# Moving two of seven block accumulations from VectorE to ScalarE and GpSimd in a fused attention and mixture-of-experts kernel

## The chip, the core and the metric

One core of a Trainium2 chip runs the whole kernel. The metric is the device time of that core in microseconds (us), as the median of several executions; lower is better. The short names of the profile are used throughout: PE is TensorE, PEld its weight loads, DVE is VectorE, ACT is ScalarE, POOL is GpSimd, SP the engine that issues most transfers.

## The reference

```python
def _attn_ref(q, k, v):                       # [8, 8, 576, 64] each
    q_p, k_p = phi(q), phi(k)                 # phi(x) = elu(x) + 1
    kv = np.einsum('bhsd,bhse->bhde', k_p, v)
    z = np.sum(k_p, axis=2)
    num = np.einsum('bhsd,bhde->bhse', q_p, kv)
    den = np.einsum('bhsd,bhd->bhs', q_p, z)[..., None] + 1e-06
    return num / den

def _moe_ref(x, w_gate, w1, w2):              # x 4608 x 512, 8 experts, F = 1024
    P = ...                                   # exp(logits), 8 rounds of row and column scaling
    out = np.zeros((N, D))
    for e in range(E):
        h = np.maximum(x @ w1[e], 0.0)
        ye = h @ w2[e]
        out += P[:, e:e + 1] * ye
    return out
# ... x is the attention's result, reshaped to 4608 x 512
```

## The kernel before

The attention runs in 16 groups, while its inputs are loaded. Then come 72 units: eight experts, nine groups of 512 tokens each. For experts 1 to 7 (63 units) the second product `h @ w2` is made by a seven-product scheme for 2 x 2 blocks, which needs sums of blocks: `S` of `h` (four for a unit) and `T` of `w2` (four for an expert). Each unit has two halves (`sub(0)`, `sub(1)`). Each half makes seven products `m1` to `m7`, and after each of them an accumulation `ev` adds the product, times the routing weight, to the output accumulator. The four sums are one DVE operation each; I call them S1 to S4.

A planner in the program (not the hardware) sets the order of the instructions on every engine. Each piece of work is a task with an estimated duration, the tasks on which it depends, and the buffers that it takes (`acq`) or uses. A dependency that crosses engines costs 0.12 us in its estimates.

```python
class _Plan:                                  # LAT = 0.12
    def slot(t):                              # when are t's buffers free?
        r = t["ready"]
        for g in t["acq"]:
            o, n = g["pool"]["order"], g["pool"]["n"]
            if len(o) >= n:
                for u in o[len(o) - n]["users"]:
                    ...
                    r = max(r, d + self.LAT)
        return r
    # ... of the tasks that can start first, the one with the lowest "prio" is taken
    # ... a finished task makes its followers ready:
    c["ready"] = max(c["ready"], t["done"] + (0.0 if list(c["eng"]) == [e] else self.LAT))

def att(b, g):                                # one of 16 attention groups
    # ... v to fp16, two casts of 64 rows
    for hh in range(2):
        def f_v(e, hh=hh):
            s = slice(64 * hh, 64 * hh + 64)
            copy(e, gvv["tile"][s, :, :, hh, 0:D], gin["v"]["tile"][s])
        tvv.append(fadd({"pool": 1.35, "dve": 0.75} if n < 2 else ("pool", 1.35), f_v, ...))
    # ...
    tqa = fadd(("none", 0.0), f_qa, deps=[tph["q"]], acq=[gq], prio=pr)      # takes the buffer of q transposed
    # ...
        t1 = fadd(("pe", 0.06 * (j1 - j0)), f_qt, deps=[tph["q"]], acq=[gp], use=[gt["q"]], prio=pr)
    # ...
    txa = fadd(("none", 0.0), f_xa, deps=[tden], acq=[gxn], prio=pr)         # takes the buffer of the result
    # ...
        t1 = fadd(("pe", 0.12 * (i1 - i0)), f_num, deps=[tden], acq=[gn], use=[gq, gz], prio=pr)

def unit(e, g, gT, tT):
    # ... layer1: h = relu(x @ w1), on PE and ACT
    for i in range(4):                        # S1..S4, one DVE tensor_tensor of 128 x 1024 each
        a0, a1, op = [(h[:, 4:8, :, 1, :], h[:, 0:4, :, 1, :], ALU.add),
                      (Sx[:, 0], h[:, 0:4, :, 0, :], ALU.subtract),
                      (h[:, 0:4, :, 0, :], h[:, 0:4, :, 1, :], ALU.subtract),
                      (h[:, 4:8, :, 0, :], Sx[:, 1], ALU.subtract)][i]
        nc.vector.tensor_tensor(out=Sx[:, i], in0=a0, in1=a1, op=op)
    def sub(s):
        def ev(region, ti, dh, dep):
            g_, col = region
            gg = 4 * g + 2 * s + ti
            def f_e(_):
                dst = acc[g][:, 2 * s + ti, 256 * dh:256 * dh + 256]
                nc.vector.scalar_tensor_tensor(out=dst, in0=g_["tile"][:, col, :], scalar=P_sb[:, gg, e:e + 1],
                                               in1=dst, op0=ALU.mult, op1=ALU.add)
            # ...
        # m1 -> e1, m5 (S1) -> e5, m2 -> ev, m6 (S2) -> e6, m3 (S4) -> ev, m7 (S3) -> e7, m4 (waits for e7) -> ev
        if e == E - 1:
            for ti in range(2):
                out_dma(g, 2 * s + ti, ...)   # two transfers for each 128 tokens, all issued by nc.sync

def out_dma(g, tt, deps):
    for half in range(2):
        ...
        nc.sync.dma_start(out=dst, in_=acc[g][64 * half:64 * half + 64, tt, :])
```

The softmax here doesn't subtract the row's maximum and nothing guards it: scores larger than these inputs give would overflow.

Of the kernel before, what the change touches and what calls it, by code (L numbers as in the profile page):

```python
# [9 lines left out]
FP32 = mybir.dt.float32  # L10
FP16 = mybir.dt.float16
AF = mybir.ActivationFunctionType
ALU = mybir.AluOpType
# [3 lines left out]
class _Plan:  # L17
# [13 lines left out]
    def add(self, eng, fn, deps=(), prio=0.0, acq=(), use=(), lat=0.0, after=0.0):  # L31

        if isinstance(eng, tuple):
            eng = {eng[0]: eng[1]}
        k = len(self.t)
        t = {"eng": eng, "fn": fn, "prio": prio, "acq": tuple(acq), "lat": lat, "kids": [], "nd": 0,
             "ready": after, "done": None, "id": k}
        self.t.append(t)
        for d in set(x for x in deps if x is not None):
            self.t[d]["kids"].append(k)  # L40
            t["nd"] += 1
        for g in list(acq) + list(use):
            g["users"].append(k)
        return k

    def run(self):
        free, avail = {}, {}
        for t in self.t:
            for e in t["eng"]:
                free.setdefault(e, 0.0)  # L50
                avail.setdefault(e, [])
            if t["nd"] == 0:
                for e in t["eng"]:
                    avail[e].append(t)
        left = len(self.t)
        end = 0.0

        def slot(t):
            r = t["ready"]
            for g in t["acq"]:  # L60
                o, n = g["pool"]["order"], g["pool"]["n"]
                if len(o) >= n:
                    for u in o[len(o) - n]["users"]:
                        d = self.t[u]["done"]
                        if d is None:
                            return None
                        r = max(r, d + self.LAT)
            return r

        while left:  # L70
            best = None
            for e, lst in avail.items():
                te = None
                for t in lst:
                    r = slot(t)
                    if r is None:
                        continue
                    s = max(free[e], r)
                    if te is None or s < te:
                        te = s  # L80
                if te is None:
                    continue
                pick = None
                for t in lst:
                    r = slot(t)
                    if r is not None and r <= te + 1e-9 and (pick is None or (t["prio"], t["id"]) < (pick["prio"], pick["id"])):
                        pick = t
                if best is None or te < best[0]:
                    best = (te, e, pick)
            assert best is not None, "plan is stuck"  # L90
            te, e, t = best
            for x in t["eng"]:
                avail[x].remove(t)
            t["start"] = te
            t["on"] = e
            free[e] = te + t["eng"][e]
            t["done"] = free[e] + t["lat"]
            end = max(end, t["done"])
            for g in t["acq"]:
                g["pool"]["order"].append(g)  # L100
            t["fn"](e)
            left -= 1
            for k in t["kids"]:
                c = self.t[k]
                c["nd"] -= 1
                c["ready"] = max(c["ready"], t["done"] + (0.0 if list(c["eng"]) == [e] else self.LAT))
                if c["nd"] == 0:
                    for x in c["eng"]:
                        avail[x].append(c)
        return end  # L110
# [3 lines left out]
def kernel(  # L114
# [10 lines left out]
    nc = tc.nc  # L125
# [6 lines left out]
    P = 128  # L132
# [9 lines left out]
    S_ = _Plan()  # L142
    add = S_.add
# [12 lines left out]
    P_sb = const.tile([P, NTT, E], FP32, tag="Pn", name="P_sb")  # L156
    NA = 7
    acc = [const.tile([P, 4, 512], FP32, tag=f"acc{g}", name=f"acc{g}") for g in range(NA)] + [None] * (NG - NA)
# [10 lines left out]
    p_t = {n: S_.pool(2) for n in "kq"}  # L169
    p_vv, p_kvz, p_qpT, p_xn, p_rden = (S_.pool(2) for _ in range(5))  # L170
    p_att, p_hq, p_h = S_.pool(2), S_.pool(2), S_.pool(2)
    p_T, p_S = S_.pool(2), S_.pool(2)
    p_w1, p_w2 = S_.pool(2), S_.pool(2)
    p_ye = [S_.pool(1) for _ in range(4)]
# [27 lines left out]
    def fadd(*a, **kw):  # L202
        t = add(*a, **kw)
        front_ids.append(t)
        return t

    def att(b, g):
        n = 2 * b + g
        pr = n - 100.0
        src = [[NJ * D, P], [2 * S * D, 2], [1, NJ * D]]  # L210
        gin, tin, gt, tph = {}, {}, {}, {}
# [8 lines left out]
        for nm in "kq":  # L220
# [15 lines left out]
            def f_m(_, ge=ge, g_=gt[nm]):  # L236
# [5 lines left out]
                       acq=[gt[nm]], use=[gin[nm]], prio=pr)  # L242
# [6 lines left out]
        ta = fadd(("none", 0.0), f_va, deps=[tin["v"]], acq=[gvv], prio=pr)  # L249
        for hh in range(2):  # L250
            def f_v(e, hh=hh):
# [3 lines left out]
                            use=[gvv, gin["v"]], prio=pr))  # L255
        gkv, gz = S_.grp(p_att), S_.grp(p_kvz)
# [17 lines left out]
        gq = S_.grp(p_qpT)  # L274
# [3 lines left out]
        tqa = fadd(("none", 0.0), f_qa, deps=[tph["q"]], acq=[gq], prio=pr)  # L278
        tq = []
        for j0, j1 in ((0, 5), (5, NJ)):  # L280
            gp = S_.grp(p_att)

            def f_qt(_, j0=j0, j1=j1, gp=gp):
                gp["tile"] = aps.tile([P, 5, 2, PW], FP16, tag="att", name="qt_ps")
                for j in range(j0, j1):
                    nc.tensor.transpose(gp["tile"][:, j - j0, :, :].rearrange("p h w -> p (h w)"),  # L286
                                        gt["q"]["tile"][:, j, :, :].rearrange("p r d -> p (r d)"), ident)

            def f_qc(e, j0=j0, j1=j1, gp=gp):
                copy(e, gq["tile"][:, :, j0:j1, :].rearrange("p h j w -> p j h w"), gp["tile"][:, 0:j1 - j0])  # L290
            t1 = fadd(("pe", 0.06 * (j1 - j0)), f_qt, deps=[tph["q"]], acq=[gp], use=[gt["q"]], prio=pr)
            tq.append(fadd({"act": 0.12 + 0.113 * (j1 - j0), "dve": 0.2 + 0.057 * (j1 - j0)}, f_qc, deps=[t1, tqa],
                           use=[gp, gq], prio=pr))
        js = [0, 2, 4, 6, 7]
# [15 lines left out]
        tden = fadd(("pe", 0.35), f_den, deps=tq + tz, acq=[gden], use=[gq, gz], prio=pr)  # L310
# [4 lines left out]
        txa = fadd(("none", 0.0), f_xa, deps=[tden], acq=[gxn], prio=pr)  # L315
        txn = []
        for i0, i1 in ((0, 2), (2, 4), (4, 5)):
            gn = S_.grp(p_att)

            def f_num(_, i0=i0, i1=i1, gn=gn):  # L320
                gn["tile"] = aps.tile([P, 2, 2, 2, D], FP32, tag="att", name="num_ps")
                for i in range(i0, i1):
                    for hh in range(2):
                        nc.tensor.matmul(gn["tile"][:, i - i0, :, hh, :],  # L324
                                         lhsT=gq["tile"][:, hh, js[i]:js[i] + 2, :].rearrange("p j w -> p (j w)"),
                                         rhs=gz["tile"][:, hh, :, 0:D], start=True, stop=True)

            def f_xn(_, i0=i0, i1=i1, gn=gn):
                nc.vector.tensor_tensor(  # L329
                    out=gxn["tile"][:, i0:i1], in0=gn["tile"][:, 0:i1 - i0].rearrange("p i r h e -> p i (r h) e"),  # L330
                    in1=grd["tile"][:, i0:i1, :, None].broadcast_to([P, i1 - i0, 4, D]), op=ALU.mult)
            t1 = fadd(("pe", 0.12 * (i1 - i0)), f_num, deps=[tden], acq=[gn], use=[gq, gz], prio=pr)
            txn.append(fadd(("dve", 0.1 + 0.28 * (i1 - i0)), f_xn, deps=[t1, trd, txa], use=[gn, grd, gxn], prio=pr))
        for c2 in range(2):
            gx = S_.grp(p_att)
# [9 lines left out]
            t1 = fadd(("pe", 0.3), f_xt, deps=txn, acq=[gx], use=[gxn], prio=pr)  # L345
# [81 lines left out]
    for b in range(B):  # L427
        att(b, 0)
        att(b, 1)
        if b % 2 == 1:  # L430
            logits(b // 2)
    p_done = sinkhorn()

    accp = []
# [11 lines left out]
    fin_prev = {}  # L446
# [87 lines left out]
    def unit(e, g, gT, tT):  # L534
        gw1, tw1, gw2, tw2 = w_t[e]
        ui = e * NG + g
# [3 lines left out]
        for i in range(4):  # L540
            def f_S(_, i=i):
                if i == 0:
# [9 lines left out]
                          use=[gh, gS], prio=ui - 399.0))  # L552
        def sub(s):
# [27 lines left out]
            def ev(region, ti, dh, dep):  # L581
                g_, col = region
                gg = 4 * g + 2 * s + ti

                def f_e(_):
                    dst = acc[g][:, 2 * s + ti, 256 * dh:256 * dh + 256]
                    nc.vector.scalar_tensor_tensor(out=dst, in0=g_["tile"][:, col, :], scalar=P_sb[:, gg, e:e + 1],  # L587
                                                   in1=dst, op0=ALU.mult, op1=ALU.add)
                t = add(("dve", 0.48), f_e, deps=[dep, fin_prev[(gg, dh)], p_done], use=[g_], prio=ui - 400.0)
                fin_prev[(gg, dh)] = t  # L590
                return t
# [63 lines left out]
```

## Time and profile before

| | before |
|---|---|
| time | 1053.62 us median of 2 runs (1053.1 to 1054.13) |
| span of the profiled execution | 1053.3 us |
| busy: PE / DVE / ACT / POOL | 1012.7 / 730.2 / 432.1 / 54.8 us |
| PE idle in 0 to 52 us | 26.5 us |
| one unit, experts 1 to 7 | 13.02 us |

The prediction below shows the lines and reads them. The front is, in what follows, the first 200 us or so, in which the attention is made and the inputs arrive.

### The profile page before, as it was taken

The numbers are of one execution on the slowest core, as the hardware profiler recorded it, in microseconds if no ns is written. First come the engines' busy times: TensorE is split into PE (matmuls) and PEld (weight loads), VectorE is DVE, ScalarE is ACT, GpSimd is POOL, SyncE is SP. The second block draws the span as 40 slices with busy tenths as digits, with TensorE's granted clock in tenths as the row PEclk, the third lists the DMA queues.
The fourth block names the chain that finished last, engine by engine and source line by source line (L and its number), as shares of the span: only waits on it lengthen the run. The fifth ranks groups of instructions, "written<-read, shape, count | busy, mean of one in ns | idle before, by whom it ended". The sixth has DMA issues, their size and how long they took to land.

```text
span 1053.3 us, 17028 instructions
## 1 busy us (share of the span) xinstructions
PE 1012.7 (96%) x7048; PEld 652.9 (62%) x7048; DVE 730.2 (69%) x1507; ACT 432.1 (41%) x693; POOL 54.8 (5%) x55
## 2 busy tenths in 40 slices
PE   2799999999999999999999999999999999999997
PEld 1455565456666666666666666666666666666664
DVE  6787876847666766667666766677666766666666
ACT  4666664453333333333333333333333333333331
POOL 3332310000000000000000000000000000000000
PEclk9999999999999999999999999999999999999999
DMA  9969600050001300050002200050003100014333
GB/s 270 326 193 248 198 6 2 1 81 2 1 1 26 56 1 1 1 81 1 1 1 41 41 1 1 1 81 1 1 1 49 32 2 1 1 28 89 83 82 81
DMA packets 31966, 55.63 MB, mean 53 GB/s; under 512 B 2704, under 2 KB 10896, under 8 KB 31888
## 3 DMA queue, kind: packets, MB, share of 16 engines
q1 hardware_dynamic: 18816, 37.76, 12.1%
q0 software_dynamic: 13072, 16.79, 9.9%
q8 instruction: 55, 0.90, 0.4%
q14 instruction: 23, 0.19, 0.1%
HBM read 61.88 MB, written 9.44 MB: 68 GB/s over the span
## 4 chain that ended last, share of the span: by engine, by line
PE 88%; DVE 7%; DMA 2%; ACT 1%; issue 1%; POOL 0%; SPq 0%; DVEq 0%; POOLq 0%; ACTq 0%
PE hq L467 45%; PE ye L576 36%; PE ye L497 4%; DMA vin<-in_v_dram 1%; DMA kin<-in_k_dram 1%; PE kv_ps L261 1%; DVE tk L239 1%; DVE xn L329 1%; DVE tq L239 1%; PE xt_ps L340 1%; PE qt_ps L286 1%; PE num_ps L324 0%; DVE ek L237 0%; DVE gs L389 0%; DVE kvz L195 0%
## 5 line engine op out<-in xcount | busy, mean ns | idle before, releaser
L471 ACT ACTIVATE h<-hq 128x512 f16<-128x512 f32 x576 | 343.4, 597 | 552.0 <-PE hq L467 551.8
L467 PE MATMUL hq<-xT,w 128*128 128x512 f16 x2304 | 556.2, 379 | 0.6 <-ACT h L471 0.6
L587 DVE SCALAR_TENSOR_TENSOR acc<-ye,P_sb,acc 128x256 f32<-128x256 f32 x882 | 396.7, 483 | 144.4 <-PE ye L576 144.4
L467 PEld LDWEIGHTS <-w 128*128 128x128 f16 x2304 | 223.9, 98 | 197.1 <-issue 1.9
L576 PEld LDWEIGHTS <-S 128*128 128x128 f16 x2016 | 197.0, 98 | 51.4 <-DVE S L550 2.2
L576 PE MATMUL ye<-T,S 128*128 128x256 f16 x1512 | 196.0, 273 | 1.2 <-DVE S L550 1.2
L576 PEld LDWEIGHTS <-h 128*128 128x128 f16 x1512 | 147.9, 98 | 58.1 <-ACT h L471 0.6
L550 DVE TENSOR_TENSOR S<-h 128x1024 f16<-128x1024 f16 x126 | 86.8, 689 | 115.4 <-ACT h L471 115.4
L576 PE MATMUL ye<-w,h 128*128 128x256 f16 x1008 | 130.8, 273 | 0.4 <-ACT h L471 0.4
L497 PE MATMUL ye<-w,h 128*128 128x512 f16 x288 | 69.7, 385 | 0.0
L576 PE MATMUL ye<-w,S 128*128 128x256 f16 x504 | 65.3, 273 | 0.2 <-DVE S L550 0.2
L576 PE MATMUL ye<-T,h 128*128 128x256 f16 x504 | 65.3, 273 | 0.1
L181 POOL DMA_DIRECT2D w<-in_moe_w_dram x16 | 13.3, 830 | 659.6 <-PE hq L467 624.3
L197 POOL CAST vv<-vin 64x1152 f16<-64x1152 f32 x32 | 40.2, 1257 | 98.7 <-PE kv_ps L261 49.5
L497 PEld LDWEIGHTS <-h 128*128 128x128 f16 x288 | 27.1, 100 | 27.5 <-issue 2.2
L550 DVE TENSOR_TENSOR S<-h,S 128x1024 f16<-128x1024 f16 x63 | 43.2, 686 | 0.0
L550 DVE TENSOR_TENSOR S<-S,h 128x1024 f16<-128x1024 f16 x63 | 42.9, 681 | 0.0
L261 PE MATMUL kv_ps<-vv,tk 128*128 128x260 f16 x144 | 22.5, 309 | 7.4 <-DVE qpT L195 5.0
L329 DVE TENSOR_TENSOR xn<-num_ps,rden 128x512 f16<-128x512 f32 (+1 forms) x48 | 26.5, 596 | 2.7 <-PE num_ps L324 1.9
L286 PE MATMUL qt_ps<-ident,tq 128*128 128x128 f16 x144 | 13.7, 235 | 14.1 <-DVE tq L239 11.0
L324 PE MATMUL num_ps<-kvz,qpT 128*128 128x128 f16 x160 | 16.0, 229 | 9.2 <-DVE xn L329 6.6
L226 ACT ACTIVATE ek<-kin 128x1152 f16<-128x1152 f32 x16 | 18.6, 1162 | 14.5 <-DMA kin<-in_k_dram 10.6
(60 smaller groups left out, 330.9 us busy)
## 6 DMA issues: line engine op xcount, KB each, us to landing
w<-in_moe_w_dram POOLq DMA_DIRECT2D x16, 1024.0 KB, 9.5
kin<-in_k_dram SPq DMA_DIRECT2D x16, 576.0 KB, 5.3
qin<-in_q_dram SPq DMA_DIRECT2D x16, 576.0 KB, 5.5
vin<-in_v_dram SPq DMA_DIRECT2D x16, 576.0 KB, 5.9
out_dram<-acc SPq DMA_DIRECT2D x72, 128.0 KB, 2.4
wg_sb<-in_moe_w_gate_dram POOLq DMA_DIRECT2D x1, 8.0 KB, 15.7
```

Of the source, the lines that this page charges most:

```text
L197: nc.gpsimd.tensor_copy(out=dst, in_=src)
L226: nc.scalar.activation(out=ge["tile"], in_=gin[nm]["tile"], func=AF.Exp)
L239: nc.vector.tensor_tensor(out=o, in0=o, in1=ge["tile"], op=ALU.max)
L261: nc.tensor.matmul(gkv["tile"], lhsT=gt["k"]["tile"][:, j, :, :].rearrange("p r d -> p (r d)"), rhs=gvv["tile"][:, :, j, :, :], start=(j = ...
L286: nc.tensor.transpose(gp["tile"][:, j - j0, :, :].rearrange("p h w -> p (h w)"), gt["q"]["tile"][:, j, :, :].rearrange("p r d -> p (r d)") ...
L329: nc.vector.tensor_tensor(out=gxn["tile"][:, i0:i1], in0=gn["tile"][:, 0:i1 - i0].rearrange("p i r h e -> p i (r h) e"), in1=grd["tile"][: ...
L467: nc.tensor.matmul(ghq["tile"], lhsT=gw1["tile"][:, c, ts(f, P)], rhs=xT[c][:, ds(512 * g, 512)], start=(c == 0), stop=(c == NDT - 1))
L471: nc.scalar.activation(out=gh["tile"][:, f, :], in_=ghq["tile"], func=AF.Relu)
L497: nc.tensor.matmul(gy[tt]["tile"], lhsT=gh["tile"][:, f, ds(P * tt, P)], rhs=gw2["tile"][:, f, :], start=(f == 0), stop=(f == NFT - 1))
L550: nc.vector.tensor_tensor(out=Sx[:, i], in0=a0, in1=a1, op=op)
L576: nc.tensor.matmul(g_["tile"][:, col, :], lhsT=lhs(kk), rhs=rhs(kk), start=(first and kk == 0), stop=(kk == 3), skip_group_check=True)
L587: nc.vector.scalar_tensor_tensor(out=dst, in0=g_["tile"][:, col, :], scalar=P_sb[:, gg, e:e + 1], in1=dst, op0=ALU.mult, op1=ALU.add)
```

## The change

The intent is to relieve DVE, the second busiest engine. Of the seven accumulations of a half unit, those of m5 and m3 (the second and fifth by program order) are split: ACT scales the product by the routing weight into a staging buffer in SBUF, and POOL adds that to the accumulator. The same change repairs two things in the planner: it counts a buffer pool that one task takes from twice, and it makes two kinds of attention tasks wait for the task that takes their buffer.

```diff
         def slot(t):
             r = t["ready"]
+            seen = {}
             for g in t["acq"]:
                 o, n = g["pool"]["order"], g["pool"]["n"]
-                if len(o) >= n:
-                    for u in o[len(o) - n]["users"]:
+                i = len(o) + seen.get(id(o), 0)
+                seen[id(o)] = i + 1 - len(o)
+                if i >= n:
+                    for u in o[i - n]["users"]:
@@
+    p_stage, ck = S_.pool(3), [0]
@@
-            t1 = fadd(("pe", 0.06 * (j1 - j0)), f_qt, deps=[tph["q"]], acq=[gp], ...
+            t1 = fadd(("pe", 0.06 * (j1 - j0)), f_qt, deps=[tph["q"], tqa], acq=[gp], ...
@@
-            t1 = fadd(("pe", 0.12 * (i1 - i0)), f_num, deps=[tden], acq=[gn], ...
+            t1 = fadd(("pe", 0.12 * (i1 - i0)), f_num, deps=[tden, txa], acq=[gn], ...
@@ def ev
+                ck[0] += 1
+                if ck[0] % 7 in (2, 5):
+                    gs_ = S_.grp(p_stage)
+
+                    def f_a(_):
+                        gs_["tile"] = accp[1].tile([P, 256], FP32, tag="stage", name="stage", bufs=3)
+                        nc.scalar.mul(out=gs_["tile"], in_=g_["tile"][:, col, :], mul=P_sb[:, gg, e:e + 1])
+
+                    def f_g(_):
+                        dst = acc[g][:, 2 * s + ti, 256 * dh:256 * dh + 256]
+                        nc.gpsimd.tensor_tensor(out=dst, in0=gs_["tile"], in1=dst, op=ALU.add)
+                    ta = add(("act", 0.5), f_a, deps=[dep, p_done], acq=[gs_], use=[g_], prio=ui - 400.0)
+                    t = add(("pool", 0.7), f_g, deps=[ta, fin_prev[(gg, dh)]], use=[gs_], prio=ui - 400.0)
+                    fin_prev[(gg, dh)] = t
+                    return ta
```

More of the change, by code (lines that the diff above doesn't have):

```diff
@@ L290, in f_qc @@
                 copy(e, gq["tile"][:, :, j0:j1, :].rearrange("p h j w -> p j h w"), gp["tile"][:, 0:j1 - j0])
-            t1 = fadd(("pe", 0.06 * (j1 - j0)), f_qt, deps=[tph["q"]], acq=[gp], use=[gt["q"]], prio=pr)
+            t1 = fadd(("pe", 0.06 * (j1 - j0)), f_qt, deps=[tph["q"], tqa], acq=[gp], use=[gt["q"]], prio=pr)
             tq.append(fadd({"act": 0.12 + 0.113 * (j1 - j0), "dve": 0.2 + 0.057 * (j1 - j0)}, f_qc, deps=[t1, tqa],
@@ L331, in f_xn @@
                     in1=grd["tile"][:, i0:i1, :, None].broadcast_to([P, i1 - i0, 4, D]), op=ALU.mult)
-            t1 = fadd(("pe", 0.12 * (i1 - i0)), f_num, deps=[tden], acq=[gn], use=[gq, gz], prio=pr)
+            t1 = fadd(("pe", 0.12 * (i1 - i0)), f_num, deps=[tden, txa], acq=[gn], use=[gq, gz], prio=pr)
             txn.append(fadd(("dve", 0.1 + 0.28 * (i1 - i0)), f_xn, deps=[t1, trd, txa], use=[gn, grd, gxn], prio=pr))
```

## The prediction

The 0.46 us of a staged copy (116 us in all, ACT about 548) is the 371 ns of the trace plus a term that is cut; without it the copies make 252 x 371 ns = 93 us and ACT 526, and the sum of the path stays 0. The 0.75 us of a POOL add (190 us, POOL about 245) came from terms that are all cut, so it was my estimate and not shown; the 0.6 to 0.75 us of blocking and the +13 to +35 us of the port rival, and through them the upper end of the range, rest on it. The point of 1053.5 us contains neither. The spacings of 215.8 and 109.2 ns are in the trace: in the unit after 621.08 us the matmuls start 215 to 216 and 109 to 110 ns apart. That they could not start sooner is not shown; what is shown is that PE has no gap to close there (200.00 us busy of 200). "The port" is my word for what the lines at 55.03 us show: the DVE sum ended 0.60 us after the end of a POOL cast (55.96 us) that had begun 0.41 us before it. That a port is the cause is not shown.

> **What bounds the kernel now.** I read the page's busy shares and slices first, then the busy times by stretch, then the chain of waits, then one unit in the timeline. One core runs, so there is one clock and no second die.
>
> The first lines of the page (engines, then the slices):
>
> ```profile
> PE 1012.7 (96%) x7048; PEld 652.9 (62%) x7048; DVE 730.2 (69%) x1507; ACT 432.1 (41%) x693; POOL 54.8 (5%) x55
> ...
> PE   2799999999999999999999999999999999999997
> ...
> PEclk9999999999999999999999999999999999999999
> ```
>
> TensorE is busy 96% of the span, at full clock; it idles in the first two slices and the last. A busy TensorE can still be a slow one, so I ask for stretches: columns are length, then busy us and instruction count of PE, PEld, DVE, ACT, POOL, then clock, DMA share and GB/s.
>
> ```profile
> 0.00:26.00 26.00, 6.99 (x47) 4.64 (x48) 17.78 (x31) 10.27 (x9) 7.95 (x13) 1.00 1.03 270
> 26.00:52.00 26.00, 18.54 (x141) 12.50 (x139) 19.24 (x36) 18.00 (x24) 9.94 (x8) 1.00 0.95 334
> ...
> 400.00:600.00 200.00, 200.00 (x1351) 132.05 (x1350) 137.77 (x285) 73.44 (x123) 3.28 (x4) 1.00 0.14 22
> 600.00:800.00 200.00, 200.00 (x1355) 132.49 (x1354) 136.62 (x283) 73.44 (x123) 1.64 (x2) 1.00 0.07 12
> ...
> 1030.00:1054.00 24.00, 15.71 (x113) 10.43 (x111) 13.50 (x29) 4.18 (x7) 0.00 (x0) 0.97 0.38 88
> ```
>
> From 200 us to the tail TensorE never idles. Its 40.6 us of idle time (1053.3 - 1012.7) are 26.5 in the first 52 us, where the DMA engines are full (share 1.03 and 0.95), about 6.5 from there to 200 us, and the rest in the tail. The chain of waits agrees: 88% PE, 7% DVE, 2% DMA. In the part that changes (63 units: experts 1 to 7, nine token groups each) the chain shows the start of each group of 12 first-layer matmuls at 256.69, 269.71, 282.73: 13.02 us for one unit.
>
> One unit in the timeline (start us, length us, engine, line, what, count, idle before):
>
> ```profile
> 623.64 0.69 DVE L550 TENSOR_TENSOR S<-h 128x1024 f16<-128x1024 f16 x1 [1.87 <-ACT h L471]
> ...
> 624.31 1.79 DVE L587 SCALAR_TENSOR_TENSOR acc<-ye,P_sb,acc 128x256 f32<-128x256 f32 x4
> 624.55 1.04 PE L576 MATMUL ye<-T,S 128*128 128x256 f16 x8
> ...
> 626.02 0.68 DVE L550 TENSOR_TENSOR S<-S,h 128x1024 f16<-128x1024 f16 x1
> ...
> 626.62 0.69 DVE L550 TENSOR_TENSOR S<-h 128x1024 f16<-128x1024 f16 x1
> 627.15 1.04 PE L576 MATMUL ye<-T,S 128*128 128x256 f16 x8
> 627.22 0.69 DVE L550 TENSOR_TENSOR S<-h,S 128x1024 f16<-128x1024 f16 x1
> ...
> 628.88 1.04 PE L576 MATMUL ye<-w,S 128*128 128x256 f16 x8
> ```
>
> These lines carry the argument. The four DVE sums S1 to S4 are made just ahead of the matmuls that load them: S4 ends at 627.91, its matmuls start at 628.88. Accumulations (L587) stand between S1 and S2.
>
> [...] A unit has 32 matmuls of 512 columns (215.8 ns) and 56 of 256 (109.2 ns): 6.91 + 6.11 = 13.02 us. The trace has exactly that, so a middle unit cannot become shorter, only longer. [...]
>
> ```profile
> 52.77 0.76 DVE L239 TENSOR_TENSOR tq<-tq,eq 128x1152 f16<-128x1152 f16 x1
> 53.41 2.54 POOL L197 CAST vv<-vin 64x1152 f16<-64x1152 f32 x2 [6.93 <-PE kv_ps L261]
> ...
> 54.46 0.46 DVE L237 TENSOR_SCALAR ek<-ek 128x1152 f16<-128x1152 f16 x1
> 55.03 1.54 DVE L239 TENSOR_TENSOR tk<-tk,ek 128x1152 f16<-128x1152 f16 x1
> ```
>
> The same two-input operation takes 0.76 us alone and 1.54 us beside a Pool cast. [...] No Pool add is in this trace; the one-input cast at 62.39 (two in 2.39 us) takes 1.19 us[...]. [...]
>
> **The change part by part.** Of seven accumulations per half unit two move, those of the products m5 and m3: 63 x 2 x 2 = 252.
>
> *Removed from DVE*: 252 x 483 ns (the L587 row) = 122 us; 730 becomes about 608 us. None of it is on the path: in the middle DVE waits for PE, not PE for DVE.
>
> *Added to ACT*: copies from PSUM take 585, 638 and 692 ns for 512, 576 and 640 columns, 0.836 ns a column, so 371 ns for 256[...]: about 0.46 us. 252 x 0.46 = 116 us; ACT becomes about 548 us (52%). It sits in gaps: ACT's 552 us of idle are waits for PE.
>
> *Added to Pool*: estimate [...]0.75 us; 252 x 0.75 = 190 us; Pool becomes about 245 us. Weight loads now stand behind adds in Pool's queue, but each weight has two buffers and an expert's time (9 x 13 = 117 us) against 9.5 us to land: hidden.
>
> *Moved order*. The compiled order shows more than the diff. In before a unit's TensorE order is m5, two first-layer groups, m6, one, m3, m7; in after one group stands before m6, so m6 and m3 come 0.87 us sooner after m5. On DVE, S1, four accumulations, S2, S3, S4 become S1, two accumulations, S2, S3, S4. Of the two repairs in the planner the repeated-slot count does nothing (no task takes two slots at once); the added dependencies reorder some attention work before 165 us, where I expect plus or minus 3 us.
>
> *The path of one unit*, with zero at the start of m5's pair and the gaps of the timeline: the two accumulations left run from -0.24 to 0.68, so S2 runs 0.60 to 1.28, S3 1.20 to 1.88, S4 1.80 to 2.48. m6 starts at 1.74 and m3 at 3.47; both are safe by 0.4 and 0.9 us. The staged copies start 0.63 (0.2 us after the product, as the L471 rows have it) and 1.07, end 1.1 and 1.55; m3, which overwrites that bank, waits for them and is safe by 1.9 us. Pool's two adds are ready near 1.2 and 1.9, just while S2 to S4 run. The sum of the planned parts on the path is therefore 0 for the middle. In the tail DVE is on the path (PE idles 1.18 us for S at 1043.25): two accumulations fewer before S2 are worth some 0.7 us, part of which the port may take back.
>
> **The rivals.** *The port becomes a wait.* If Pool's adds get in both between S2 and S3 and between S3 and S4 (each blocking some 0.6 to 0.75 us), S4 ends at 2.48 + 1.2 to 1.5 = 3.7 to 4.0, past 3.47: TensorE stalls 0.2 to 0.55 us a unit, 63 units: +13 to +35 us. For it: the lines at 55.03[...], and the packed order. Against it: the first add is ready only as S3 is being issued; if S3 wins, at most one add stands before S4, which then ends near 3.2, in time. I give the full form 3 chances in 10.
>
> *ACT becomes the bound or blocks TensorE.* A staged copy waits at the head of ACT's queue, with activations behind it. Against: 52% load, and the copies stand in the order in which TensorE finishes, with four banks for first-layer results. It would show as PE waiting for ACT; 1 in 20, some +5 us.
>
> *DVE relief pays.* DVE at 69% looks like a second bottleneck. Against: TensorE is at its rate in the middle, so nothing can be gained but in front and tail: 1 to 3 us, of 34 us idle which the input loads or the tail's data set. 2% would be 21 us.
>
> **Range and chances.** The central case is 1053.6 of before, minus about 0.5 in the tail, front unknown by 3: 1050 to 1056. To this comes the port rival with 3 in 10 and +13 to +35 us, its lower half inside the range that I state. Point 1053.5, range 1048.5 to 1068; faster by over 2% 0.01, slower by over 2% (over 0.33 us a unit) 0.13, the rest within.
>
> **What would show it right or wrong.** Right: counts DVE 1255, ACT 945, POOL 307; DVE near 608 us, unit spacing still 13.02 us, PE without idle between 200 and 1030 us. The steps: mean of an add near 0.75 us (longer if it is blocked), of the staged copy near 0.46 us; L550 above 0.69 us shows the port lock. Wrong: PE idle before the matmuls with S, released by DVE, some tenths of a us in each unit and a spacing above 13.2 us (the port), or released by ACT (the staged copy); or slices before 165 us whose PE busy time differs by more than 3 us (the reordered front).

## The result

| | before | after |
|---|---|---|
| time, us | 1053.62 (1053.1 to 1054.13, 2 runs) | 1058.12 (1057.27 to 1058.96, 2 runs) |
| span of the profiled execution, us | 1053.3 | 1057.2 |
| PE idle ahead of matmuls, us | 34.9 | 39.2 |
| DVE / ACT / POOL busy, us | 730.2 / 432.1 / 54.8 | 655.3 / 541.6 / 294.0 |

The ratio of the times is 1.0042, with a 95% interval from 1.0017 to 1.0066: the same within 2%, but a small, real loss. A ratio here is always the mean time of one kernel's fast runs over that of the other's of the same rounds, so it is not quite the ratio of the medians quoted.

The page of the kernel after: the engines' busy times with their instruction counts, then the first row of the slices.

```profile
PE 1011.4 (96%) x7048; PEld 652.7 (62%) x7048; DVE 655.3 (62%) x1251; ACT 541.6 (51%) x949; POOL 294.0 (28%) x307
...
PE   2699999999999999999999999999999999999996
```

DVE lost 75 us of work and nothing came of it: PE is as busy as before, with the same number of matmuls. The second slice and the last fell by one tenth each. So the loss is to be looked for mainly at the two ends.

Groups of the page of the kernel after, among its costliest: the columns are line, engine and operation, tiles, shapes and count, then busy us, mean ns of one, and the idle time before them.

```profile
L599 POOL TENSOR_TENSOR acc<-stage,acc 128x256 f32<-128x256 f32 x252 | 237.7, 963 | 546.7 <-ACT stage L595 546.7
...
L595 ACT ACTIVATE stage<-ye,P_sb 128x256 f32<-128x256 f32 x252 | 114.8, 475 | 52.1 <-PE ye L580 51.8
...
L554 DVE TENSOR_TENSOR S<-h,S 128x1024 f16<-128x1024 f16 x63 | 76.6, 1217 | 0.0
```

The last row is S4. On the page of the kernel before it is this row:

```profile
L550 DVE TENSOR_TENSOR S<-h,S 128x1024 f16<-128x1024 f16 x63 | 43.2, 686 | 0.0
```

Before it took 686 ns and 43.2 us in all, now 1217 ns and 76.6 us; S1, S2 and S3 stay between 679 and 694 ns. The extra 0.53 us falls on S4 alone, in every unit: its shortest record of 63 is 1214 ns, its longest 1220. The timeline of one unit of the kernel after shows why (start us, length us, engine, line, what, count, idle before):

```profile
627.89 1.04 PE L580 MATMUL ye<-T,S 128*128 128x256 f16 x8
628.50 0.68 DVE L554 TENSOR_TENSOR S<-S,h 128x1024 f16<-128x1024 f16 x1
...
629.10 0.68 DVE L554 TENSOR_TENSOR S<-h 128x1024 f16<-128x1024 f16 x1
629.14 2.35 POOL L599 TENSOR_TENSOR acc<-stage,acc 128x256 f32<-128x256 f32 x2 [8.14 <-ACT stage L595]
...
629.70 1.22 DVE L554 TENSOR_TENSOR S<-h,S 128x1024 f16<-128x1024 f16 x1
...
631.37 1.04 PE L580 MATMUL ye<-w,S 128*128 128x256 f16 x8
```

The staged copy frees POOL's first add at 629.14, 0.04 us after S3 has started. The add has to wait for S3, S4 has to wait for the add, and the second add waits for S4: the two engines take turns, in all 63 units (S4 ends 0.55 us after the end of the first add, the second add 0.58 to 0.59 us after the end of S4). (The prediction's lines at 55.03 us show the like between a DVE sum and a POOL cast, 1.54 us in place of 0.76; from here on it is called the lock on the port.) S4 ends at 630.92; its matmuls (m3, the last line) start at 631.37. So 0.45 us are left, no PE time is lost, and the units still start 13.02 us apart.

The tail is different. The timeline of the last unit of the kernel after, then the same part of the kernel before (the SPq line is the issue of eight output transfers):

```profile
1047.50 1.05 PE L580 MATMUL ye<-w,S 128*128 128x256 f16 x8 [0.69 <-DVE S L554]
1048.20 0.91 ACT L595 ACTIVATE stage<-ye,P_sb 128x256 f32<-128x256 f32 x2 [2.21 <-PE ye L580]
...
1048.76 1.41 POOL L599 TENSOR_TENSOR acc<-stage,acc 128x256 f32<-128x256 f32 x2 [0.73 <-ACT stage L595]
...
1049.51 4.96 SPq L486 DMA_DIRECT2D out_dram<-acc  x8
```

```profile
1044.32 2.58 DVE L587 SCALAR_TENSOR_TENSOR acc<-ye,P_sb,acc 128x256 f32<-128x256 f32 x6
1044.46 1.05 PE L576 MATMUL ye<-w,S 128*128 128x256 f16 x8 [0.16 <-DVE S L550]
1045.34 1.04 PE L576 MATMUL ye<-T,S 128*128 128x256 f16 x8
1045.62 4.97 SPq L482 DMA_DIRECT2D out_dram<-acc  x8
```

The eight matmuls with a weight as operand (`ye<-w,S`) are m3 of the last unit, both halves. From their start to the first output issue it takes 1045.62 - 1044.46 = 1.16 us before, when one DVE instruction lies between, and 1049.51 - 1047.50 = 2.01 us after, when an ACT copy and a POOL add do. From that issue on the two traces agree: eight issues in a row, 0.62 us each, and the end of the span 7.7 us after the first (1053.30 and 1057.16). The last issue waits for the seven ahead of it, not for the last accumulation, so a later first issue is a later end.

With gaps ahead of matmuls taken from the two traces, and the time after the last matmul (5.75 us before, 6.50 after), the difference of the spans, 3.9 us, is made up like this, as the gaps have it:

| part | after minus before, us |
|---|---|
| PE idle, 0 to 52 us | +3.5 |
| PE idle, 110 to 170 us | +0.7 |
| PE idle at the first unit with accumulations, near 243 us | +0.5 |
| PE idle in the tail | -0.2 |
| after the last matmul | +0.75 |
| PE's own busy time (1012.7 to 1011.4) | -1.3 |

The first and the last row belong together: the first 52 us hold 25.54 us of PE work before and 22.08 after, in a front with another order, and TensorE runs at half clock there for most of the time (matmuls of 128 columns 107 ns apart in place of 56, next section), so that busy and idle time say little by themselves. Starting times in the two traces give a sum without that. The first first-layer matmul starts at 44.08 us before and 45.86 after (+1.78). From it to the first routing matmul (`lg_ps`) both take 116.17 us. From there to the first first-layer matmul of the first unit with accumulations it is 71.96 and 72.89 (+0.93), from that to the next unit's 13.02 and 13.65 (+0.63), to the last unit nothing is added, and from the last S1 to the end it is 13.02 and 13.53 (+0.51). Together that is 3.85 of the 3.86 us.

### The profile page after: what moved, and what is told of

Read it like the earlier page. It is cut to its first block, busy times and chain, and to the rows that moved or that the text cites. A ratio compares the mean times of both kernels' runs of the same rounds, so it can differ in the third digit from the quotient of the medians.

```text
span 1057.2 us, 17661 instructions
## 1 busy us (share of the span) xinstructions
PE 1011.4 (96%) x7048; PEld 652.7 (62%) x7048; DVE 655.3 (62%) x1251; ACT 541.6 (51%) x949; POOL 294.0 (28%) x307
## 4 chain that ended last, share of the span: by engine, by line
PE 87%; DVE 9%; DMA 2%; issue 1%; ACT 1%; SPq 0%; DVEq 0%; ACTq 0%
PE hq L471 45%; PE ye L580 36%; PE ye L501 3%; DMA kin<-in_k_dram 2%; DVE tk L243 1%; DVE xn L333 1%; PE kv_ps L265 1%; PE xt_ps L344 1%; DVE tq L243 1%; PE qt_ps L290 1%; DVE ek L241 1%; DVE eq L241 1%; DVE S L554 0%; DVE tq L236 0%; DVE gs L393 0%
## 5 line engine op out<-in xcount | busy, mean ns | idle before, releaser
L599 POOL TENSOR_TENSOR acc<-stage,acc 128x256 f32<-128x256 f32 x252 | 237.7, 963 | 546.7 <-ACT stage L595 546.7
L607 DVE SCALAR_TENSOR_TENSOR acc<-ye,P_sb,acc 128x256 f32<-128x256 f32 x630 | 286.1, 481 | 166.2 <-PE ye L580 166.1
L595 ACT ACTIVATE stage<-ye,P_sb 128x256 f32<-128x256 f32 x252 | 114.8, 475 | 52.1 <-PE ye L580 51.8
L554 DVE TENSOR_TENSOR S<-h,S 128x1024 f16<-128x1024 f16 x63 | 76.6, 1217 | 0.0
L501 PEld LDWEIGHTS <-h 128*128 128x128 f16 x288 | 27.0, 100 | 27.1 <-issue 2.3
```

The lines of the kernel that those rows point to most:

```text
L501: nc.tensor.matmul(gy[tt]["tile"], lhsT=gh["tile"][:, f, ds(P * tt, P)], rhs=gw2["tile"][:, f, :], start=(f == 0), stop=(f == NFT - 1))
L595: nc.scalar.mul(out=gs_["tile"], in_=g_["tile"][:, col, :], mul=P_sb[:, gg, e:e + 1])
L599: nc.gpsimd.tensor_tensor(out=dst, in0=gs_["tile"], in1=dst, op=ALU.add)
```

## A second level in the times, which is not the change

Runs of one kernel fall on two levels some 1.5 us apart: among the experiments before took 1052.7 to 1053.4 or 1054.4 to 1054.6, after 1057.3 to 1057.6 or 1058.3 to 1059.0. A difference of one microsecond can be read only between runs of one level. The traces show what separates them. The timeline of the kernel after, profiled at 1058.96 us, and then that of the experiment off_only, profiled at 1054.15 us, at the same point of the program (L361 makes the routing logits, 8 columns a matmul):

```profile
167.79 2.84 PE L361 MATMUL lg_ps<-wg_sb,xT 128*128 128x8 f16 x108
170.50 5.30 PE L501 MATMUL ye<-w,h 128*128 128x512 f16 x16
```

```profile
165.54 2.85 PE L361 MATMUL lg_ps<-wg_sb,xT 128*128 128x8 f16 x108
168.24 3.61 PE L501 MATMUL ye<-w,h 128*128 128x512 f16 x16
```

The same 16 matmuls take 5.30 us or 3.61: 1.69 us. In the first case the clock records of the trace have 0.50 for 3.413 us, from 171.25 to 174.67 us, and 1.00 before and after; half the clock for 3.413 us is 1.71 us. It fell right after 108 matmuls of 8 columns in 2.85 us, in which PE shows no gap. Of 13 profiled executions, four have this stretch (before at 1055.08, after at 1058.96 and 1058.95, n0_split at 1051.71), each with 1.70 to 1.72 us lost by the granted clock; each is on the upper level of its kernel. The other nine do not have it, and those of them whose kernel showed two levels are on the lower.

That the narrow matmuls bring it about is my reading; no run took them away. The traces support it further. In each of them the recorded changes of the clock in mid-run lie whole multiples of 3.413 us, the length of the stretch itself, after the moment at which the full clock begins for good (before: 45.68 us, and 36 times 3.413 us later 168.56; after: 44.96 us, and 37 times later 171.25), so windows of this length can be counted from there. In the four executions with the stretch, the 108 narrow matmuls fill 2.56 to 2.71 us of the window just ahead of it; in the other nine they fall across the windows so that none has more than 2.34 us of them.

The traces show one thing more about the clock, which the clock column hides, because it reads 1.00 wherever no record exists. Two lines of timelines of the kernel before, five matmuls of 128 columns each:

```profile
39.61 0.74 PE L340 MATMUL xt_ps<-ident,xn 128*128 128x128 f16 x5
...
50.76 0.44 PE L340 MATMUL xt_ps<-ident,xn 128*128 128x128 f16 x5
```

In all 13 executions such matmuls stand some 107 ns apart until the full clock begins, at 42.5 to 47.7 us, and 56 ns apart after it; four executions have one window at full clock in between, near 25 to 31 us. So TensorE runs most of its first 42.5 to 47.7 us at half clock, in every kernel here.

The first profiles of before and after both have the stretch near 170 us, so the 3.9 us between their spans are not touched by it. In what follows I give the ratio over all fast runs, and beside it the medians of the lower level. For before that is 1053.0 us, for after 1057.5: a loss of 4.5.

## The experiments

Eleven kernels ran, beside the kernel before on the same chip, all correct. The theory after the result (A in the expectations) was: the change in the middle costs nothing, since the port takes back 0.53 us per unit that are not on the path; the loss comes from the reordered front (the two added dependencies) and, in smaller part, from the handoff ahead of the first output. The rival was that the offload itself costs the time somewhere.

### The offload alone, without the two dependencies: off_only

```diff
-            t1 = fadd(("pe", 0.06 * (j1 - j0)), f_qt, deps=[tph["q"], tqa], acq=[gp], ...
+            t1 = fadd(("pe", 0.06 * (j1 - j0)), f_qt, deps=[tph["q"]], acq=[gp], ...
-            t1 = fadd(("pe", 0.12 * (i1 - i0)), f_num, deps=[tden, txa], acq=[gn], ...
+            t1 = fadd(("pe", 0.12 * (i1 - i0)), f_num, deps=[tden], acq=[gn], ...
```

> The moved accumulations alone, with the planner's dependencies of the kernel before. Theory A (the loss is the planner's reordering of the front, plus a longer last handoff): front as before, S1 of the first unit near 233 us instead of 235.8, unit spacing 13.02 us, S4 at 1.22 us; only the tail is longer by about 0.5 us; time about 1054 to 1055, ratio to before 1.0005 to 1.001. Theory B (the offload itself costs, by the shared port): as the changed kernel, ratio 1.003 to 1.005.

Measured: 1054.25 us (1054.15 to 1054.53) against 1053.11 for before, ratio 1.0007 [0.9995, 1.002], by itself not told from no change. By the lower level it is +1.25. The front is back: PE idles 26.7 us in the first 52, as before (26.5), and the first first-layer matmul starts at 43.64 us (before 44.08, after 45.86). S4 still takes 1.216 us and units are still 13.02 us apart. The part of the loss that belongs to the offload shows in two places. One is the tail (5.88 us from the last S1 to the first output issue of the last group, before 5.34). The other is the first unit, in the timeline of off_only:

```profile
236.60 2.13 POOL L599 TENSOR_TENSOR acc<-stage,acc 128x256 f32<-128x256 f32 x2 [1.11 <-ACT stage L595]
236.94 1.22 DVE L533 TENSOR_TENSOR T<-w 128x1024 f16<-128x1024 f16 x1
...
238.60 0.60 PE L580 MATMUL ye<-T,h 128*128 128x256 f16 x4 [0.47 <-DVE acc L607]
```

Here a T sum of the weights falls beside the second pair of adds and is stretched from 0.68 to 1.22 us, the accumulation of m7 behind it comes late, and m4, which has to wait for that accumulation, costs PE 0.47 us. T is made once for an expert. The four sums at this place are those for expert 2, made back to back; those for the experts 3 to 7 stand 1.7 to 2.2 us apart, none takes over 0.80 us, and none makes a gap. By starting times this unit takes 13.65 us instead of 13.02, and from the last S1 to the end it is 13.54 instead of 13.02: with 0.63 and 0.52 us these two places hold 1.15 of the 1.25 us.

### The dependencies alone: deps_only

```diff
-            t1 = fadd(("pe", 0.06 * (j1 - j0)), f_qt, deps=[tph["q"]], acq=[gp], ...
+            t1 = fadd(("pe", 0.06 * (j1 - j0)), f_qt, deps=[tph["q"], tqa], acq=[gp], ...
-            t1 = fadd(("pe", 0.12 * (i1 - i0)), f_num, deps=[tden], acq=[gn], ...
+            t1 = fadd(("pe", 0.12 * (i1 - i0)), f_num, deps=[tden, txa], acq=[gn], ...
```

(The edit is on the kernel before; nothing else of the change is in.)

> The kernel before with both added dependencies and no offload. Theory A (the planner's reordering is most of the loss): ratio 1.002 to 1.0035, TensorE idle up by 1.7 to 3.5 us in the first 52 us and by 0.7 us from 110 to 170 us, no idle at the first unit, tail as before. Theory B (the offload is the loss): ratio 1.000.

Measured: 1055.91 us (1055.58 to 1057.4, 6 runs) against 1053.09, ratio 1.0027 [1.0015, 1.004]; lower level 1055.6, +2.6. PE idle in 0 to 52 us is 29.1 (before 26.5), in 110 to 170 it is 2.9 (2.2). So the repair of the planner, which adds no instruction at all, is the larger part of the loss: 2.6 of 4.5, the offload 1.25, and 0.6 stay that neither accounts for. In the traces these 0.6 us lie ahead of the first routing matmul, which starts at 161.46 us here and at 162.04 and 162.03 in the two traces of the kernel after, although the engines' order up to there is the same. The five traces with exactly the front's order of before spread from 159.58 to 160.25 at this point, so the 0.6 may be no effect of the change at all.

### Which group's dependency: txa_n0 and txa_rest

The compiled order had shown that the first dependency (on `tqa`) changes nothing and the second everything; the traces agree, for PE's order in deps_only is that of txa_rest with the exchange of txa_n0 at its beginning. These two runs ask in which of the 16 attention groups it costs.

```diff
 # txa_n0
-            t1 = fadd(("pe", 0.12 * (i1 - i0)), f_num, deps=[tden], acq=[gn], ...
+            t1 = fadd(("pe", 0.12 * (i1 - i0)), f_num, deps=[tden] + ([txa] if n == 0 else []), acq=[gn], ...
 # txa_rest: the same with n > 0
```

> The kernel before with the added dependency on the xn buffer for the very first attention group alone: in the compiled order it exchanges the first num_ps and the second kv_ps and nothing after. Theory A1 (that first exchange is what loses the front): first-layer work starts near 45.9 us instead of 44.1, time about 2 us over before (ratio 1.002). Theory A2 (the later reorderings at 80 to 165 us lose it): ratio 1.000.

Measured: 1054.85 us (1054.7 to 1056.34), ratio 1.0019 [1.0005, 1.0033]; lower level 1054.8, +1.8. PE idle in 0 to 52 us is 28.2, against 26.5; later stretches as before.

> The kernel before with the added dependency for all groups but the first: the order is as before until the eighth group, then differs. Theory A1: ratio 1.000 (within 0.7 us). Theory A2: about 2.5 us over before (ratio 1.0025).

Measured: 1053.54 us (1053.41 to 1055.27), ratio 1.0003 [0.9991, 1.0016]; lower level 1053.5, +0.5. Its idle in 110 to 170 us is 2.9 instead of 2.2, and the first 52 us are as before.

So one dependency in the first group costs most. What it does: `txa` is a task without an engine, and the planner adds its 0.12 us latency ahead of the followers. By that hair the second group's `kv_ps` wins a PSUM buffer over the first group's `num_ps`, and goes ahead of it on PE. Everything behind it shifts: the first first-layer matmul starts at 45.44 us; in the six traces without this exchange, and with the casts of before, it starts at 43.29 to 44.08. From there to the routing both kinds take the same 116.0 to 116.2 us.

### The offload, except in the last unit: off_notlast

```diff
 # on off_only
-                if ck[0] % 7 in (2, 5):
+                if ck[0] % 7 in (2, 5) and not (e == E - 1 and g == NG - 1):
```

> As off_only, but the last of the 63 units accumulates on DVE alone. If the tail's loss is the handoff from ACT to Pool ahead of the first output transfer of the last group, the output issues start 0.5 to 0.8 us earlier than in off_only relative to the last S1 (5.3 us after it as before, not 5.9), and time is that of before within 0.5 us. If the tail's loss is elsewhere, no difference to off_only.

Measured: 1053.76 us (1053.46 to 1055.14), ratio 1.0004 [0.9992, 1.0017]; lower level 1053.7, 0.5 below off_only. In the trace the interval from the last S1 to the first output issue is 5.34 us, exactly that of before, where off_only has 5.88. The trace confirms the handoff in the tail; the time agrees, though 0.5 us is within the spread of the runs.

### The kernel after once more: after_again

No edit: this checks the loss with more runs and gives a second trace.

> The changed kernel itself, timed on the same chip as the next runs and with more rounds: ratio near 1.004. TensorE idle in the first 52 us is 29.9 us in its first profile against 28.2 us in the run with the first exchange alone, whose order there is the same: if that is spread of the transfers' arrival, this profile lies anywhere from 28 to 30; if something of the offload costs it, near 29.9 again.

Measured: 1058.32 us (1057.47 to 1058.95, 5 runs) against 1053.09 (10 runs), ratio 1.0043 [1.0029, 1.0057]. PE idle is 37.8 us in all, against 39.2 in the first trace, and yet the spans are 1057.18 and 1057.16: here the half clock lasted until 47.7 us instead of 45.0, and slower matmuls fill part of the idle time (23.6 us of PE work in the first 52 us, against 22.1). PE's idle time in the front is thus not a measure of the loss by itself.

### Is it the lock on the port, and where does it begin to cost? off_hold

POOL is kept busy longer on purpose, just ahead of its first add: it copies the staged tile eight times over (2048 elements) into a scratch buffer that nobody reads. The output stays correct.

```diff
 # on off_only
+                    n5 = ck[0] % 7 == 2 and s == 0
                     def f_g(_):
+                        if n5:
+                            junk = accp[1].tile([P, 8, 256], FP16, tag="junk", name="junk", bufs=1)
+                            nc.gpsimd.tensor_copy(out=junk, in_=gs_["tile"][:, None, :].broadcast_to([P, 8, 256]))
```

> The offload alone, with one more Pool instruction ahead of the first add of each unit: a copy of the staged tile, repeated eight times, to a scratch tile that nobody reads (2048 elements[...]). Port theory: it takes the port as S3 ends and holds it; S4, which waits, grows from 1.22 to about 2.4 us and ends some 0.7 us after its matmuls could start; units are 13.02 + 0.6 to 0.8 us and the time is 1092 to 1105 us. If the port is shared and not locked, or S4's matmuls have more slack than I read, S4 grows little and the time stays below 1058 us.

Measured: 1104.81 us (1104.68 to 1104.97), ratio 1.0487 [1.0472, 1.0501]. Units are 13.79 us apart, +0.77. The timeline of off_hold:

```profile
621.30 2.40 POOL L602 CAST junk<-stage 128x2048 f16<-128x2048 f32 x1 [7.76 <-ACT stage L595]
...
621.87 2.38 DVE L554 TENSOR_TENSOR S<-h,S 128x1024 f16<-128x1024 f16 x1
...
624.31 0.39 PE L580 MATMUL ye<-w,S 128*128 128x256 f16 x2 [0.60 <-DVE S L554]
```

S4 is stretched to 2.38 us and ends at 624.25, 0.55 us after the copy ends at 623.70: it ran only then. The matmuls that load it stall for 0.60 us. S4 is 1.16 us longer than beside the add (1.22), of which the slack of 0.45 us absorbs a part; 0.71 are left by this sum, and the unit grew by 0.77. That shows the mechanism: what POOL has begun at this place is put in whole ahead of S4. By the same sum, an estimate from these two traces, an add longer by 0.45 us would begin to cost, 63 times over. The rival "the offload costs in the middle" falls for the kernel as it is: 0.45 us of slack cover it.

### Two issue queues for the last outputs: b_twoq

If eight issues of 0.62 us in a row set the end, then two queues should shorten it, with or without the change. This edit is on the kernel before.

```diff
-                nc.sync.dma_start(out=dst, in_=acc[g][64 * half:64 * half + 64, tt, :])
+                (nc.scalar if g == NG - 1 and half == 1 else nc.sync).dma_start(
+                    out=dst, in_=acc[g][64 * half:64 * half + 64, tt, :])
```

> The kernel before with the last group's eight output transfers issued from two queues, alternately SP and ACT. If the tail is bound by one queue's issues (eight in a row from 1045.6 to 1050.6 us, each about 0.63 us, the last ready piece at 1048.1), the end comes 1.5 to 2.5 us sooner (ratio 0.998). If it is bound by the last accumulation and the landing time, no difference.

Measured: 1052.63 us (1051.64 to 1053.43, 4 runs), ratio 0.9991 [0.9977, 1.0005], not told from no change by the time. The trace does tell: from the last S1 to the end it takes 11.83 us, before 13.02. The timeline of b_twoq:

```profile
1043.35 3.15 SPq L482 DMA_DIRECT2D out_dram<-acc  x4
1043.36 3.42 ACTq L482 DMA_DIRECT2D out_dram<-acc  x4
...
1044.89 0.92 DVE L588 SCALAR_TENSOR_TENSOR acc<-ye,P_sb,acc 128x256 f32<-128x256 f32 x2 [0.25 <-PE ye L577]
```

The issues end 1.5 us sooner than in one queue, but 1.2 us is all that is won, less than the 1.5 to 2.5 that I expected: now the last issues wait for the last accumulation (1044.89 + 0.92), which had been hidden before. The chain of issues bound the tail, and behind it, 1.2 us away, stands the next bound.

### Shorter POOL casts in the front: b_split and n0_split

The prediction's own lines show a two-input DVE operation that waits 0.78 us beside a POOL cast of 1.34 us. If DVE waits for whatever POOL has begun, shorter POOL instructions should make the waits shorter. Theory P was that txa_n0 loses because of more such collisions (in its first 52 us blocked DVE operations have 6.2 us of extra time, before 3.7), so that the split takes the loss away; theory Q was that the PE order itself costs it.

```diff
 # b_split, on the kernel before; n0_split is the same edit on txa_n0
-                copy(e, gvv["tile"][s, :, :, hh, 0:D], gin["v"]["tile"][s])
+                for r in range(2):
+                    copy(e, gvv["tile"][s, r, :, hh, 0:D], gin["v"]["tile"][s, r])
```

> The kernel before with each Pool cast of v cut in two (64 x 576 instead of 64 x 1152, same order of everything). Port theory: a blocked VectorE operation waits for one Pool instruction at most, so the time lost by blocked VectorE operations in the first 52 us falls from 3.7 us to about 2; the time falls by 0 to 1 us. Otherwise: no change, or slower by the casts' doubled fixed cost[...].

Measured: 1048.53 us (1048.17 to 1048.89, 5 runs) against 1052.87, ratio 0.9957 [0.9943, 0.9972]. That is 4.3 us by an edit of one line, more than I expected (0 to 1 us of it, and in the wrong stretch). The busy times by stretch of the kernel before, then of b_split, for 52 to 110 and 110 to 170 us (length, then busy us and count of PE, PEld, DVE, ACT, POOL, then clock, DMA share, GB/s):

```profile
52.00:110.00 58.00, 53.95 (x466) 33.01 (x465) 46.58 (x92) 40.41 (x57) 17.66 (x15) 1.00 0.76 217
110.00:170.00 60.00, 57.78 (x608) 36.48 (x607) 45.61 (x87) 37.01 (x59) 9.41 (x8) 0.99 0.24 74
```

```profile
52.00:110.00 58.00, 56.50 (x485) 34.61 (x484) 46.55 (x96) 42.74 (x58) 24.22 (x30) 1.00 0.82 229
110.00:170.00 60.00, 59.64 (x615) 37.62 (x614) 44.04 (x93) 35.54 (x59) 10.19 (x12) 1.00 0.19 62
```

PE's idle time in these 118 us falls from 6.3 to 1.9 us: the whole gain. Most of it is one wait, that of `num_ps` for DVE's `xn` (L329 before, L330 here), which falls from 4.3 to 1.0 us. PE waits for no cast there in either trace, so it is not that the halves of a cast are ready sooner for PE. Over 52 to 160 us, blocked DVE operations lose 3.8 us in place of 9.4. POOL itself does more work than before (its page rows: 32 casts with 40.2 us busy become 64 with 50.8), and that costs nothing. The first 52 us gain little: PE idles 26.8 us there, where the inputs are still arriving (DMA share 0.99).

> The kernel with the first exchange alone, its casts cut in two as well. Theory P (the exchange loses time because six VectorE operations fall beside Pool casts and wait for the port, 6.2 us in place of 3.7): the extra over b_split falls to about 1 us (ratio of the two 1.001) and the blocked time to about 3.2 us. Theory Q (it loses time by TensorE's order itself, the second kv_ps ahead of the first num_ps): the extra over b_split stays near 1.9 us.

Measured: 1051.71 us (1050.38 to 1052.1), ratio 0.9983 [0.997, 0.9996]; lower level 1050.45, against 1048.5 for b_split: +1.9. That is the cost of the one dependency without the split as well (+1.8), and it lies ahead of the first first-layer matmul (43.96 us in b_split, 45.78 here), although blocked DVE operations in the first 52 us now lose 3.0 us, about as in b_split (2.7). Theory P falls. The loss goes with the order on PE, theory Q; which wait in that order carries it stays open, for the edit also moves small tasks between DVE and ACT (in all, one more on ACT). (The clock column has 0.50 from 30 to 40 us in b_split and 1.00 in n0_split, but that is the missing record: such matmuls stand 107 ns apart in both. Two executions of off_only with mean clocks of 0.991 and 0.999 took 1054.25 and 1054.15 us.)

### The best version: b_split_twoq

The split casts and the two queues together, on the kernel before, without the offload.

> The kernel before with the casts cut in two and the last outputs on two queues: the sum of the two gains, if both are: 1051 to 1052.5 us (ratio 0.998 to 0.9995).

Measured: 1047.25 us (1046.26 to 1049.62, 5 runs) against 1052.87, ratio 0.9947 [0.9934, 0.996], better than expected, for b_split had not yet shown its 4.3 us. It beats the kernel before by 5.6 us and the kernel after by about 11.

### All runs

PE idle is the sum of the gaps ahead of matmuls in the trace, in us, without the time after the last one; where a field is empty it plays no part in the argument.

| kernel | median us (runs) | ratio to before | PE idle 0-52 | 52-170 | 225-1030 |
|---|---|---|---|---|---|
| before (profile of the start) | 1053.62 (2) | 1 | 26.5 | 6.3 | 0 |
| after | 1058.12 (2) | 1.0042 | 29.9 | 6.9 | 0.5 |
| after_again | 1058.32 (5) | 1.0043 | 28.4 | 7.0 | 0.5 |
| off_only | 1054.25 (5) | 1.0007 | 26.7 | 6.3 | 0.5 |
| off_notlast | 1053.76 (5) | 1.0004 | 27.1 | 6.3 | 0.5 |
| deps_only | 1055.91 (6) | 1.0027 | 29.1 | 7.0 | 0 |
| txa_n0 | 1054.85 (5) | 1.0019 | 28.2 | 6.3 | 0 |
| txa_rest | 1053.54 (5) | 1.0003 | 26.8 | 7.0 | 0 |
| off_hold | 1104.81 (4) | 1.0487 | | | 36.6 |
| b_twoq | 1052.63 (4) | 0.9991 | | | 0 |
| b_split | 1048.53 (5) | 0.9957 | 26.8 | 1.9 | 0 |
| n0_split | 1051.71 (5) | 0.9983 | 28.9 | 1.9 | 0 |
| b_split_twoq | 1047.25 (5) | 0.9947 | 27.1 | 1.9 | 0 |

## Why the prediction was right, and where it was off

The time fell in the middle of the stated range and within 2%, and the main argument held: nothing is won in the middle, and the lock on the port costs nothing there. But that it fell into the range was partly luck. The prediction's central case was 1050 to 1056 us, and 1058.12 lies above it; the range reached further only for the port rival's stalls, which did not come, while the loss came from the front and the edges. The point was 4.6 us too low, and these are the steps, in the prediction's order.

**The bound and the path of one unit held.** A unit takes 13.02 us before and after. The sum "0 for the middle" is what the runs show, up to 0.63 us at the first unit (0.47 of it a gap), where the prediction had "PE without idle between 200 and 1030 us". The term left out there is the T sums: beside POOL's adds one of them takes 1.22 us in place of 0.68. I had looked only at S. "At full clock" was misread for the first 46 us: the clock column has no record there, and TensorE ran at half clock (matmuls of 128 columns 107 ns apart, later 56).

**"252 x 483 ns = 122 us; 730 becomes about 608": 655 was measured.** Two terms were wrong. The row's mean was multiplied by the count although successive accumulations overlap: the group's busy time is 396.7 us for 882, 0.45 each, and it fell by 396.7 - 286.1 = 110.6 us. And S4 took back 76.6 - 43.2 = 33.4 us by waiting for POOL. That leaves -77, and -75 was measured. The mistake cost nothing, since DVE is not on the path.

**ACT and POOL held in size.** The staged copy took 475 ns for "about 0.46"; ACT 541.6 us for 548. A POOL add that nobody blocks took 0.70 us (two in 1.41 us, in the tail) for "0.75"; the mean of 963 ns holds the waits for DVE, so POOL came to 294 us, not 245. Counts were 1251, 949 and 307 for 1255, 945 and 307: in the reordered front the planner gave four small tasks to ACT instead of DVE.

**The port rival came in the half form that the text described.** "At most one add stands before S4, which then ends near 3.2" after the start of m5: it ended at 630.92 - 627.89 = 3.03, and m3 started at 3.48. Its full form, put at 3 in 10, did not come, because the engines take turns: S3, add, S4, add. off_hold shows what it would have cost, and that the slack was only 0.45 us.

**"Plus or minus 3 us" for the front was the step that failed in sign.** I took the reordering as noise around zero. Here it lost each time: deps_only costs 2.6 us, txa_n0 alone 1.8 and txa_rest 0.5 (of which the interval of its ratio includes no change). That a front which had been tuned in one order is more likely to lose than to gain by an accidental other one is a guess. The prediction's own sign of it came: PE is busy 3.5 us less in the first 52 us. The compiled order was there to see before the run; I read how many lines moved, but not that the second group's work went ahead of the first's.

**The tail was wrong in sign.** "Two accumulations fewer before S2 are worth some 0.7 us" is true for S2, whose wait fell from 1.18 to 0.34 us. But S4 then costs 0.69 us where it had cost 0.16, and the first output issue waits for a chain of two engines instead of one. After the last matmul it takes 0.75 us more, with -0.2 ahead of it: +0.5, not -0.5.

**"DVE relief pays" was rightly given little.** DVE lost 75 us of busy time, and not a microsecond of the span followed from it. Where DVE does hold PE up, in the front, the cure was not less work on DVE but shorter work on POOL (b_split). The prediction had put the front's idle time down to the input loads; 4.4 us of it, between 52 and 170 us, went when the POOL casts were cut.

Open remain 0.6 of the 4.5 us, which neither half of the change shows alone and which may be spread, and the wait through which the order of txa_n0 loses its 1.8 us.

## What to carry to other kernels

Work taken off an engine that nothing waited for was worth nothing here, while its replacement cost at the edges: one handoff more ahead of the first output, and one more POOL instruction that a DVE sum waits for (S4 took 1.22 us in place of 0.69), with a slack that has to be measured (here 0.45 us, in 63 units). A repair in a planner is a change of the schedule even if it adds no instruction, so compare the compiled order and run it alone. Where two-input DVE work and POOL work share a stretch, try shorter POOL instructions: here that one line was worth 4.3 us, the opposite sign of the whole change.
